# A two-layer feed-forward behind a chunked scan: layer 1's high part rounded by VectorE from ScalarE's result, and the first piece's diagonal copies on VectorE alone

## The chip, the cores and the metric

One core of a Trainium2 chip. The metric is the device time of one execution in microseconds (us), the median of several runs. Of the core's engines the text names TensorE (PE), VectorE (DVE), ScalarE (ACT), GpSimd (POOL) and SyncE (SP), which here issues the data DMAs.

## The reference

Inputs: x (4 x 8 x 768 x 32), decays a (4 x 8 x 768), B and C (4 x 8 x 768 x 16), and the weights of two layers. First comes attention as a decayed linear scan over chunks of 32 positions; then two feed-forward layers over 3072 tokens of 256 values, 2048 hidden ones.

```python
for c in range(nc):                       # chunks of 32 positions
    cum = np.cumsum(la, axis=-1)          # la = log of the clipped decays
    L = np.exp(cum[:, :, :, None] - cum[:, :, None, :]) * causal
    y_intra = np.einsum('bhij,bhjd->bhid', np.einsum('bhin,bhjn->bhij', Cc, Bc) * L, xc)
    y_inter = np.einsum('bhin,bhnd->bhid', Cc, state) * np.exp(cum)[:, :, :, None]
    y[:, :, sl] = y_intra + y_inter
    state = decay_full[:, :, None, None] * state + np.sum(Bx, axis=2)
x = y.transpose(0, 2, 1, 3).reshape(B * S, H * D)
h = x @ w_in1;  x = np.maximum(0.01 * h, h) @ w_out1        # layer 1
h = np.maximum(x @ w_in2, 0.0);  out = (h * h) @ w_out2     # layer 2
```

## The kernel before, in words

**Numbers in two parts.** The layers multiply in a rounded format (`float32r`, fp32r in the rows). Each fp32 number is kept as a high part, rounded to that format, and a low part, what the rounding leaves; a product is three matmuls: low by high, high by high, high by low. So whoever makes an operand makes two: `yh` and `yl` (input of a layer), `gh` and `gl` (hidden values), `wh` and `wl` (weights).

**Weights.** They arrive as 8-byte numbers, four matrices (`1i`, `1o`, `2i`, `2o`: layer, in or out) of eight chunks each. A chunk is loaded (`load_w`), turned into fp32 by two ACT operations (L130, L133, `split_w`) and two DVE operations (L141, L142, `split_w1`), then cut into parts by ACT (L153) and DVE (L154, `split_w2`). Weight chunks are worked on from the start to some 160 us.

**Pieces, blocks, tiles.** The 3072 tokens are twelve pieces of 256, three to each of four sequences. `scan_piece` (L308) is a generator that scans one piece in some twenty steps: scales and decays (`decays`, L189; `from_start`, L195), a block-diagonal copy of each operand (`diag`, L314, into `kbd`, `xbh`, `xbl`, `sbd`), matmuls into `S` and `Y`, the states `stt` (L213) carried from piece to piece, their halves `shl` (L382, L384), transposed to `t16` (L386), and at the end `yh` (L397, ACT) and `yl` (L398, DVE). `diag` moves four quadrants of 32 partitions: in piece 0 by engines, two on DVE and two on ACT for each of the four operands; in later pieces by four SP DMAs (L318). Behind that a block is one piece (the first four) or two (the last four). A block passes layer 1, then layer 2, in the written order `ORDER`, whose entries are layer and block: block 0, 1 and 2 of layer 1, then block 0 of layer 2, and so on in turn.

A block's hidden values come in tiles of 128 x 512 (`t`, `gh`, `gl`, three buffers each), 8 to a one-piece block, 96 to a layer. `hmm` (L417) makes the 12 matmuls of a tile into PSUM (three buffers), `act` (L429) makes the hidden values of it on ACT and DVE, and `omm` (L445), two or three tiles later (`LAG`), multiplies them by the out weights: lines 453 and 454 with `gh`, L458 with `gl`. `finish` (L460) hands the result on as layer 2's `yh`, `yl` (L466, L467) or writes it out (L471, L472).

In layer 1 `act` is: ACT reads PSUM twice, once rounding to `gh` (L435), once to fp32 `t` (L436); DVE forms `gl` as their difference (L441). In layer 2 ACT makes `t` (L438), DVE squares it (L439), ACT rounds it to `gh` (L440), DVE forms `gl` (L441).

**What sets the order.** The program interleaves these steps by its own counters: `step_to(due(...))` advances the scan so that a block's pieces are ready in time, `w_step` the weight chunks. The scales of a later sequence (`sequence_scales`, L269) are stepped beside the scan: five loads of `all` (L276, one buffer, on SP) and a square of each on ACT (L235). A tile framework then gives each engine one static queue, which it works through in order; where its scheduler puts an instruction depends on the others, so an edit of a line also moves lines that it does not touch.

Of the kernel before, what the change touches and what calls it, by code (L numbers as in the profile page):

```python
# [15 lines left out]
AF = mybir.ActivationFunctionType  # L16
# [29 lines left out]
def ssd_moe_kernel(ctx: ExitStack, tc: tile.TileContext, in1, in2, w1i, w1o, w2i, w2o, out):  # L46
# [6 lines left out]
    nc = tc.nc  # L53
# [254 lines left out]
    def scan_piece(p, tiles, get_y):  # L308
# [5 lines left out]
        def diag(dst, src):  # L314
            for h in range(4):
                d, v = dst[quad[h], :, h, :], src[quad[h]]
                if p > 0:
                    nc.sync.dma_start(d, v)  # L318
                else:
                    (nc.vector.tensor_copy if h < 2 else nc.scalar.copy)(d, v)  # L320

        him = sp.tile([P, U, T], F16, tag="f0", name="him")
        ch = sp.tile([P, U, T], F16, tag="f2", name="ch")
# [6 lines left out]
        cl = sp.tile([P, U, T], F16, tag="f3", name="cl")  # L330
        nc.vector.scalar_tensor_tensor(kmx, bt_t, sb, him, ALU.mult, ALU.subtract)
        diag(kbd, kmx)
        xh = sp.tile([P, U, D], F16, tag="xh", name="xh")
        nc.scalar.activation(xh, x_t, AF.Copy, scale=sx)
# [5 lines left out]
        xl = sp.tile([P, U, D], F16, tag="xl", name="xl")  # L340
        nc.vector.scalar_tensor_tensor(xl, x_t, sx, xh, ALU.mult, ALU.subtract)
        diag(xbh, xh)
        yield
        mkh = sp.tile([P, U, T + N], F16, tag="mkh", name="mkh")
        mkl = sp.tile([P, U, T + N], F16, tag="mkl", name="mkl")
        S = pz.tile([P, U, T], F32, tag="S", name="S")
        for u in range(U):
# [6 lines left out]
            mk[:, :, T:], b_t, sb, lt[:, :, T - 1 : T].to_broadcast([P, U, N]), ALU.mult, ALU.mult  # L354
        )
        diag(xbl, xl)
        yield
        nc.vector.scalar_tensor_tensor(mk[:, :, :T], S, kk, lt, ALU.mult, ALU.mult)
# [47 lines left out]
    class Phase:  # L406
# [22 lines left out]
        def act(self, ms):  # L429
            n, hp = self.n, self.h  # L430
            t = ap_.tile([P, 512], F32, tag="t", name="t", bufs=3)
            gh, gl = (ap_.tile([P, 512], F32R, tag=x, name=x, bufs=3) for x in ("gh", "gl"))
            if self.layer == 1:

                nc.scalar.activation(gh, hp, AF.Lrelu)  # L435
                nc.scalar.activation(t, hp, AF.Lrelu)  # L436
            else:
                nc.scalar.activation(t, hp, AF.Relu)  # L438
                nc.vector.tensor_tensor(t, t, t, ALU.mult)  # L439
                nc.scalar.copy(gh, t)  # L440
            nc.vector.tensor_tensor(gl, t, gh.bitcast(F32), ALU.subtract)  # L441
            for j, m in enumerate(ms):
                self.g[m] = gh[:, j * n : j * n + n], gl[:, j * n : j * n + n]
# [176 lines left out]
```

## Time and profile before

| | us |
|---|---|
| median of 3 runs | 636.08 (635.6 to 636.33) |
| the profiled execution | 637.78 |
| its span (first to last instruction) | 636.1 |
| PE busy | 586.2 (92%) |
| DVE busy, 687 instructions | 402.6 (63%) |
| ACT busy, 678 instructions | 372.9 (59%) |
| mean granted clock of PE | 0.99 of full speed |

The span is cut into stretches below, since the shares over the whole do not hold in each: the first layer-1 block starts at 31.65 us, all weight chunks are done near 160, and the scan ends much before the layers do. Where a row gives an idle time in brackets, it is the engine's idle time just ahead of the row's instruction, with the releaser that the trace infers.

### The profile page before, as it was taken

To read this page: it belongs to the slowest core of one execution; us is meant where nothing else is said; L and a number is where in the kernel's file an instruction comes from. 1 tells how busy PE (TensorE), PEld (TensorE's weight loads), DVE (VectorE), ACT (ScalarE), POOL (GpSimd) and SP (SyncE) were. 2 spreads that over 40 slices of the span, in tenths; PEclk is the share of its full clock that TensorE was granted. 3 is DMA by queue.
4 is the path that set the end of the run, shared out by engine and by line. 5 is a ranking of instruction groups with operands and counts; after the bars stand their busy time and mean duration, and the time that the engine had idled before them with its cause. 6 is when DMAs were issued, how large, how long until landed. Compare 5 with 4: busy or idle time off the path is not lost.

```text
span 636.1 us, 11298 instructions
## 1 busy us (share of the span) xinstructions
PE 586.2 (92%) x4434; PEld 516.9 (81%) x4434; DVE 402.6 (63%) x687; ACT 372.9 (59%) x678; POOL 5.2 (1%) x14
## 2 busy tenths in 40 slices
PE   0297698999989999999999999999999999999997
PEld 0287698989989888899988888888888888888885
DVE  6999999995558664576564576564565322555553
ACT  6999998876555545545545555455544433544442
POOL 3000000000000000000000000000000000000000
PEclk9999898999989999999999999999999999999999
DMA  7886565555351412202212212212000000000000
GB/s 272 275 291 195 139 205 98 174 124 127 105 94 40 74 51 26 50 35 42 51 51 26 49 36 25 51 67 26 9 1 9 34 1 1 0 2 0 34 1 33
DMA packets 111396, 46.47 MB, mean 73 GB/s; under 512 B 94320, under 2 KB 101104, under 8 KB 111344
## 3 DMA queue, kind: packets, MB, share of 16 engines
q1 hardware_dynamic: 111344, 45.76, 27.8%
q8 instruction: 35, 0.57, 0.4%
q14 instruction: 17, 0.14, 0.1%
HBM read 36.83 MB, written 3.15 MB: 63 GB/s over the span
## 4 chain that ended last, share of the span: by engine, by line
PE 76%; ACT 9%; DVE 6%; DMA 6%; issue 2%; SPq 1%; DVEq 0%; ACTq 0%
PE o L453 12%; PE hp L425 12%; PE hp L427 12%; PE hp L426 12%; PE o L458 12%; PE o L454 12%; DMA all<-in 2%; DMA in<-in 2%; ACT wst L130 1%; ACT wst L133 1%; ACT sq L235 1%; SPq L318 1%; ACT t L436 1%; ACT gh L435 1%; DVE e L195 1%
## 5 line engine op out<-in xcount | busy, mean ns | idle before, releaser
L441 DVE TENSOR_TENSOR gl<-t,gh 128x512 fp32r<-128x512 f32 x192 | 132.3, 689 | 139.5 <-ACT t L436 85.9
L435 ACT ACTIVATE gh<-hp 128x512 fp32r<-128x512 f32 x96 | 57.2, 596 | 84.1 <-PE o L454 75.6
L425 PE MATMUL hp<-yl,wh1i 128*128 128x256 f32 (+1 forms) x256 | 89.5, 350 | 10.8 <-DVE yl L398 4.6
L440 ACT CAST gh<-t 128x512 fp32r<-128x512 f32 x96 | 59.5, 620 | 66.3 <-DVE t L439 56.2
L439 DVE TENSOR_TENSOR t<-t 128x512 f32<-128x512 f32 x96 | 66.2, 689 | 43.4 <-ACT t L438 43.1
L438 ACT ACTIVATE t<-hp 128x512 f32<-128x512 f32 x96 | 57.4, 598 | 56.7 <-PE hp L427 54.5
L453 PE MATMUL o<-gh,wl1o 128*128 128x256 f32 (+1 forms) x256 | 84.9, 347 | 4.5 <-DVE wl1o L154 3.6
L426 PE MATMUL hp<-yh,wh1i 128*128 128x256 f32 (+1 forms) x256 | 88.6, 346 | 0.0
L427 PE MATMUL hp<-yh,wl1i 128*128 128x256 f32 (+1 forms) x256 | 88.4, 345 | 0.0
L426 PE MATMUL hp<-yh,wh2i 128*128 128x256 f32 (+1 forms) x256 | 86.0, 336 | 0.0
L425 PE MATMUL hp<-yl,wh2i 128*128 128x256 f32 (+1 forms) x256 | 86.0, 336 | 0.0
L427 PE MATMUL hp<-yh,wl2i 128*128 128x256 f32 (+1 forms) x256 | 86.0, 336 | 0.0
L453 PE MATMUL o<-gh,w2o 128*128 128x256 f32 (+1 forms) x256 | 83.6, 343 | 1.6 <-DVE yl L467 1.5
L454 PE MATMUL o<-gh,wh1o 128*128 128x256 f32 (+1 forms) x256 | 83.0, 340 | 0.0
L454 PE MATMUL o<-gh,w2o 128*128 128x256 f32 (+1 forms) x256 | 81.9, 336 | 0.0
L425 PEld LDWEIGHTS hp<-yl,wh1i 128*128 128x128 f32 x256 | 51.3, 200 | 16.7 <-DVE ss L256 3.8
L458 PE MATMUL o<-gl,wh1o 128*128 128x256 f32 (+1 forms) x256 | 60.5, 339 | 0.0
L458 PE MATMUL o<-gl,w2o 128*128 128x256 f32 (+1 forms) x256 | 60.3, 336 | 0.0
L453 PEld LDWEIGHTS o<-gh,wl1o 128*128 128x128 f32 x256 | 48.9, 191 | 10.6 <-DVE wl1o L154 4.7
L436 ACT ACTIVATE t<-hp 128x512 f32<-128x512 f32 x96 | 57.1, 594 | 0.0
L426 PEld LDWEIGHTS hp<-yh,wh1i 128*128 128x128 f32 x256 | 51.3, 200 | 5.1 <-issue 0.3
L427 PEld LDWEIGHTS hp<-yh,wl1i 128*128 128x128 f32 x256 | 51.0, 199 | 5.1
(123 smaller groups left out, 984.8 us busy)
## 6 DMA issues: line engine op xcount, KB each, us to landing
in<-in SPq DMA_DIRECT2D x12, 640.0 KB, 4.6
in<-in SPq DMA_DIRECT2D x12, 512.0 KB, 3.4
all<-in SPq DMA_DIRECT2D x15, 384.0 KB, 3.7
wst<-w1i SPq DMA_DIRECT2D x8, 512.0 KB, 7.9
wst<-w1o SPq DMA_DIRECT2D x8, 512.0 KB, 5.8
wst<-w2o SPq DMA_DIRECT2D x8, 512.0 KB, 5.1
wst<-w2i SPq DMA_DIRECT2D x8, 512.0 KB, 4.7
out_t<-ob SPq DMA_DIRECT2D x8, 256.0 KB, 2.2
```

Of the source, the lines that this page charges most:

```text
L425: nc.tensor.matmul(hp, wh, self.xl[:, :, k], start=(k == 0), stop=False)
L426: nc.tensor.matmul(hp, wh, self.xh[:, :, k], start=False, stop=False)
L427: nc.tensor.matmul(hp, wl, self.xh[:, :, k], start=False, stop=(k == KI - 1))
L435: nc.scalar.activation(gh, hp, AF.Lrelu)
L436: nc.scalar.activation(t, hp, AF.Lrelu)
L438: nc.scalar.activation(t, hp, AF.Relu)
L439: nc.vector.tensor_tensor(t, t, t, ALU.mult)
L440: nc.scalar.copy(gh, t)
L441: nc.vector.tensor_tensor(gl, t, gh.bitcast(F32), ALU.subtract)
L453: nc.tensor.matmul(self.o[d], wl, gh, start=(m == 0), stop=False)
L454: nc.tensor.matmul(self.o[d], wh, gh, start=False, stop=False)
L458: nc.tensor.matmul(self.o[d], wh, gl, start=False, stop=(m == KO - 1))
```

## The change

In `act`, for layer 1, ACT reads PSUM once, into `t`, and DVE rounds `t` to `gh` by a copy into the rounded format. In `diag`, for piece 0, all four quadrants go by DVE copies. No other line is touched.

```diff
@@ L317 (diag, piece 0)
-                    (nc.vector.tensor_copy if h < 2 else nc.scalar.copy)(d, v)
+                    nc.vector.tensor_copy(d, v)
@@ L432 (Phase.act, layer 1)
-                nc.scalar.activation(gh, hp, AF.Lrelu)
                 nc.scalar.activation(t, hp, AF.Lrelu)
+                nc.vector.tensor_copy(gh, t)
```

So 96 ACT operations of 128 x 512 and 8 of 32 x 512 leave ACT, and as many come to DVE. In the changed kernel L435 is the ACT operation that makes `t`, and L436 the DVE copy, named CAST. The queues move as well; three places follow.

DVE, in the scan of piece 0 (`in_117` holds that piece's products, `e_179` its decays from the start). One piece of the difference, - before, + after:

```order
 L320 COPY kbd<-kmx 32x16x32 x2
 L189 SCALAR_TENSOR_TENSOR lt<-in_117,delta 128x512
-L320 COPY xbl<-xl 32x16x32
+L320 COPY kbd<-kmx 32x16x32 x2
+L320 COPY xbh<-xh 32x16x32 x2
 L353 SCALAR_TENSOR_TENSOR in_117<-in_116,sc,lt 128x16x16
-L320 COPY xbl<-xl 32x16x32
+L320 COPY xbl<-xl 32x16x32 x4
+L358 SCALAR_TENSOR_TENSOR in_117<-S,kk,lt 128x16x32
 L368 SCALAR_TENSOR_TENSOR ql<-e_179,sc,qh 128x512
```

The copies that ACT made stand in DVE's queue, among DVE's own, all ahead of the first `yl`.

DVE, in front of block 2's `yl` (the third L398), of before and then of the change (`in_1280` and `in_1279` are inputs of piece 3):

```order
L441 TENSOR_TENSOR gl<-t,gh 128x512
L350 TENSOR_TENSOR e_1561<-in_1279,e_1561 128x512
L341 SCALAR_TENSOR_TENSOR xl<-in_1279,sc,xh 128x512
L142 SCALAR_TENSOR_TENSOR wst<-wst 128x512
L205 MEMSET d1s 128x32
L141 SCALAR_TENSOR_TENSOR wst<-wst 128x512
L331 SCALAR_TENSOR_TENSOR kmx<-in_1280,sc,him 128x512
L398 SCALAR_TENSOR_TENSOR yl<-Y,fac,yh 128x512
```

```order
L436 CAST gh<-t 128x512
L154 TENSOR_TENSOR wl2i<-wst,wh2i 128x2x256
L441 TENSOR_TENSOR gl<-t,gh 128x512
L141 SCALAR_TENSOR_TENSOR wst<-wst 128x512
L195 SCALAR_TENSOR_TENSOR e_1561<-in_1280,d1e 128x512
L142 SCALAR_TENSOR_TENSOR wst<-wst 128x512
L341 SCALAR_TENSOR_TENSOR xl<-in_1279,sc,xh 128x512
L350 TENSOR_TENSOR e_1561<-in_1279,e_1561 128x512
L154 TENSOR_TENSOR wl2i<-wst,wh2i 128x2x256
L398 SCALAR_TENSOR_TENSOR yl<-Y,fac,yh 128x512
L331 SCALAR_TENSOR_TENSOR kmx<-in_1280,sc,him 128x512
```

Each layer-1 `gl` has a CAST ahead of it now, and one operation that stood in front of this `yl`, L331, stands behind it.

ACT, around piece 4's `shl`, of before and then of the change (`ob` is layer 2's output of a block, `sq` the square of a load `all`, `d1s` and `stt` are the states of piece 4):

```order
L471 COPY ob<-o_1984 128x256
L325 ACTIVATE ch<-in_2509,sc 128x512
L235 ACTIVATE sq,mx<-all 128x768
L435 ACTIVATE gh<-hp 128x512
L436 ACTIVATE t<-hp 128x512
L435 ACTIVATE gh<-hp 128x512
L436 ACTIVATE t<-hp 128x512
L377 ACTIVATE d1s<-Y 128x32x8
L235 ACTIVATE sq,mx<-all 128x768
L382 CAST shl<-stt 128x16x16
L207 ACTIVATE d1s<-stt 128x32
```

```order
L471 COPY ob<-o_1984 128x256
L235 ACTIVATE sq,mx<-all 128x768
L435 ACTIVATE t<-hp 128x512 x2
L235 ACTIVATE sq,mx<-all 128x768
L377 ACTIVATE d1s<-Y 128x32x8
L382 CAST shl<-stt 128x16x16
L207 ACTIVATE d1s<-stt 128x32
L235 ACTIVATE sq,mx<-all 128x768
L435 ACTIVATE t<-hp 128x512
```

Before, two squares stand between `ob` and `shl`, the second of them directly ahead of `shl`; now the two stand ahead of `d1s`, and a third stands behind `shl`.

## Rows read from the trace of the kernel before

**Rows 1.** page, its sections 1 and 4: engines' busy time, and the chain that ended last

```profile
PE 586.2 (92%) x4434; PEld 516.9 (81%) x4434; DVE 402.6 (63%) x687; ACT 372.9 (59%) x678; POOL 5.2 (1%) x14
...
PE 76%; ACT 9%; DVE 6%; DMA 6%; issue 2%; SPq 1%; DVEq 0%; ACTq 0%
```

**Rows 2.** busy time by stretch: length, then us busy (instructions) of each engine, granted clock, DMA

```profile
12.28:30.85 18.57, 4.26 (x112) 3.90 (x112) 17.95 (x34) 18.46 (x33) 0.00 (x0) 1.00 0.78 262
30.85:72.68 41.83, 31.85 (x308) 29.46 (x308) 41.40 (x89) 41.81 (x85) 0.00 (x0) 1.00 0.74 225
72.68:104.00 31.32, 28.91 (x308) 28.22 (x308) 30.00 (x61) 28.82 (x55) 0.00 (x0) 0.95 0.64 167
...
104.90:160.00 55.10, 53.56 (x542) 53.15 (x543) 45.33 (x76) 40.83 (x77) 0.00 (x0) 0.97 0.51 129
220.00:632.00 412.00, 411.91 (x2589) 347.98 (x2587) 219.22 (x336) 200.47 (x352) 0.00 (x0) 1.00 0.12 26
```

**Rows 3.** timeline of PE: start, us, line, operation, idle before and releaser

```profile
73.46 0.39 PE L425 MATMUL hp<-yl,wh1i 128*128 128x256 f32 x1 [3.68 <-DVE ss L256]
...
104.89 0.51 PE L425 MATMUL hp<-yl,wh1i 128*128 128x256 f32 x1 [2.16 <-DVE yl L398]
...
137.70 0.39 PE L453 MATMUL o<-gh,w2o 128*128 128x256 f32 x1 [1.54 <-DVE yl L467]
...
179.75 0.18 PE L393 MATMUL Y<-qh,sbd 128*128 128x32 f16 x1 [2.93 <-DMA sbd<-t]
```

**Rows 4.** timeline of DVE before the second and third `yl`

```profile
71.55 1.21 DVE L189 TENSOR_TENSOR_SCAN lt<-in,delta 128x512 f32<-128x512 f32 x1
72.68 0.72 DVE L398 SCALAR_TENSOR_TENSOR yl<-Y,fac,yh 128x512 fp32r<-128x512 f32 x1
...
100.26 0.68 DVE L441 TENSOR_TENSOR gl<-t,gh 128x512 fp32r<-128x512 f32 x1
100.86 0.68 DVE L350 TENSOR_TENSOR e<-in,e 128x512 f32<-128x512 f32 x1
...
103.34 0.74 DVE L331 SCALAR_TENSOR_TENSOR kmx<-in,sc,him 128x512 f16<-128x512 f32 x1
104.00 0.74 DVE L398 SCALAR_TENSOR_TENSOR yl<-Y,fac,yh 128x512 fp32r<-128x512 f32 x1
```

**Rows 5.** busy time by stretch, PE alone: us, us busy, granted clock, DMA

```profile
104.90:108.90 4.00, 4.00 (x21) 0.57 0.42 44
137.00:141.00 4.00, 3.30 (x26) 1.00 0.56 114
179.70:183.70 4.00, 3.95 (x47) 0.57 0.39 43
```

**Rows 6.** groups of ACT: count, us busy, mean ns; the last from 104.9 to 160 alone

```profile
L435 ACT ACTIVATE gh<-hp 128x512 fp32r<-128x512 f32 x96 | 57.2, 596 | 84.1 <-PE o L454 75.6 <-PE hp L427 8.4
L320 ACT COPY kbd<-kmx 32x512 f16<-32x512 f16 x2 | 1.2, 611 | 0.0
...
L435 ACT ACTIVATE gh<-hp 128x512 fp32r<-128x512 f32 x9 | 5.4, 601 | 4.3 <-PE hp L427 4.1
```

**Rows 7.** groups of DVE over the whole span

```profile
L441 DVE TENSOR_TENSOR gl<-t,gh 128x512 fp32r<-128x512 f32 x192 | 132.3, 689 | 139.5 <-ACT t L436 85.9 <-ACT gh L440 53.1
L186 DVE TENSOR_SCALAR in<-in 128x496 f32<-128x496 f32 x12 | 4.9, 411 | 0.0
L320 DVE COPY kbd<-kmx 32x512 f16<-32x512 f16 x2 | 0.6, 283 | 0.0
```

**Rows 8.** timeline of ACT ahead of piece 4's `shl`

```profile
168.15 0.39 ACT L377 ACTIVATE d1s<-Y 128x256 f32<-128x256 f32 x1
172.54 0.84 ACT L235 ACTIVATE sq<-all 128x768 bf16<-128x768 f32 x1 [4.01 <-DMA all<-in]
173.39 0.66 ACT L382 CAST shl<-stt 128x256 f16<-128x256 f32 x1
```

**Rows 9.** timeline of SP's DMA queue, piece 4's `sbd`

```profile
175.54 2.61 SPq L318 DMA_DIRECT2D sbd<-t  x4
```

## The prediction

> **What bounds the kernel now.** The page's first lines give TensorE (PE) 586.2 of the span's 636.1 us, VectorE (DVE) 402.6 and ScalarE (ACT) 372.9, and the chain that ended last is 76% PE [rows 1]. Read over the whole span, that says PE. The busy times by stage [rows 2] say it differently. From 220 us on PE is busy 411.91 of 412.00, and DVE and ACT have slack (219.22 and 200.47). Before 104 us it is the other way: between 30.85 and 72.68 PE works 31.85 of 41.83 us, while DVE is busy 41.40 and ACT 41.81. Over the three stretches from 12.28 to 104.00 DVE is idle 0.62, 0.43 and 1.32, together 2.37 us. In that front DVE and ACT scan the first pieces and split weights, and PE waits.
>
> So the question is when PE is fed, and the timeline of PE shows it [rows 3]. The first matmuls of layer 1's blocks 1 and 2 begin at 73.46 and 104.89, after idle times of 3.68 and 2.16 us. The releaser of the latter is the `yl` of the block's piece (L398), the last instruction of its scan; the former is put down to a small DVE operation just behind a `yl`. DVE's timeline [rows 4] shows the third and second `yl` at 104.00 and 72.68, with the next operation in front of each starting 0.66 and 1.13 us earlier, that is, without a gap. Hence the start of block 2 is the sum of all that stands in DVE's queue ahead of the third `yl`. Behind block 2 PE seldom waits; what it waits for longest there is one DMA at 179.75, for 2.93 us [rows 3]. That stall is the second place that matters.
>
> A further cost hangs on such idle times. In the four microseconds after the gaps of 2.16 and 2.93 the granted clock is 0.57, and after a gap of 1.54 at 137.70 it is 1.00 [rows 5]. At 0.57 in the mean, 4 us do the work of 2.3: each of the two gaps costs 1.7 us more.
>
> **The change part by part.** *What leaves ACT*: 96 `gh` (L435) of 596 ns and the eight copies of the first piece (L320), 611 ns each [rows 6]. What of this lies behind 220 us is worth nothing, since PE is the bound there. In the front ACT loses 8 x 0.61 = 4.9 us, and up to 0.60 us a tile. That pays only so far as DVE waited for ACT, at most the 2.37 us of idle time above.
>
> *What comes to DVE, the diagonal copies.* The copies it already makes take 283 ns [rows 7]. Eight more, at 0.28, are +2.24 us, all ahead of the first `yl`.
>
> *What comes to DVE, the cast of `t` to `gh`.* The trace of before has no such DVE operation. Nearest above: L441, of the same size and in SBUF, but with two inputs, 689 ns. Nearest below: L186, one input, fp32 in SBUF, 496 columns wide, 411 ns [rows 7]. As L441 is followed after 0.60 us (100.26 to 100.86 in [rows 4]), 0.09 overlap, so in a full queue the cast costs between 0.33 and 0.60. I take 0.34, since one input and its memory are what it shares with L186. The Trainium skill, "VectorE: DVE Perf Modes", section "The perf-mode tier table", has copies of fp32 in SBUF run at twice the rate of a two-input operation; by that the sum is the one below, and by L441's row the third `yl` would come another 16 x 0.26 = 4.2 us later.
>
> *The sum at each `yl`.* I counted DVE's queue ahead of each, before and after the change. First `yl`: +2.24, less two L142 that have moved behind it (0.60 each): +1.0. Second: +2.24, plus 8 casts (2.72), less one scan of a later piece, L189 (1.13), that has moved behind it: +3.8. Third: +2.24, plus 16 casts (5.44), less two L141 and one L142 (1.80) and one L331 (0.66): +5.2. Of this the relieved ACT can give back up to 2.37. How much is not shown; I take half, 1.2. **Block 2 starts 4.0 us later, between +2.9 and +5.2**, near 108.9. Behind its start PE's order is the same but for one tile, so the delay stays. The weight splits that move back are layer 2's, whose first block comes only after block 2.
>
> From block 2 to 220 us DVE gets another cast a tile. It is busy 45.33 of 55.10 us from 104.90 to 160 [rows 2] and PE runs there nearly without a wait, so the casts of that stretch (9 tiles of layer 1 by ACT's groups [rows 6], 3.1 us) and the few splits that have moved back fit into its 9.8 idle ones; ACT gives up as many `gh` there, so `t` is not later. I count this at nothing. If the cover is gone, the wait at 137.70 (DVE's `yl`, L467) grows by a cast or two, +0.3 to +0.7.
>
> *What comes back at the DMA stall.* PE waits at 179.75 for `sbd` of piece 4. Its chain stands in ACT's timeline [rows 8]: ACT is ready for `shl` (L382) after `d1s` at 168.15, yet the next in its queue is a square whose load (`all`, one buffer) arrives at 172.54, after 4.01 us of idling; `shl` runs at 173.39, and SP issues the four `sbd` at 175.54 [rows 9]. In the changed order that square stands behind `shl`, and on SP one load fewer stands ahead of `sbd`. Then `shl` is set by the later of `d1s`, which ends at 168.54 and has one DVE scan behind it, and the previous square; so up to 4 us are to be had. But the previous square's load is now issued behind the two output DMAs, and other operations of ACT have moved too. I take 1.5 to 3 us of the 4. A gap of 2.93 becomes 0 to 1.4; with 1.4 or less the clock stays (as after 1.54). The return lies between 0 and 2.93 + 1.7 = 4.6; I take 2.0, under half, as the queue shift is certain and its size is not.
>
> Sum: +4.0 - 2.0 = +2.0 on a profiled execution of 637.78 us, which lies 1.7 us above the median of 636.08. Against the median that is 638.1; **I say 638.0**.
>
> **The rivals.**
>
> *A. The front's loss stays, a part comes back* (the forecast, slower): between +2.9 - 1.6 and +5.2 - 0.9, that is +1.3 to +4.3: 637.4 to 640.4. For it: DVE without a gap to 72.68 [rows 2]. The Trainium skill has a rule that speaks against the change in the same sense: "Perfetto Trace Analysis", section "Optimizing Scalar/DVE Operations", says that where VectorE is saturated, giving some of its work to ScalarE may make sense; the change does the reverse where VectorE is at 41.40 of 41.83.
>
> *B. Given back at the stall* (no change): +4.0 in front, and 3 to 4.6 back, as the gap falls to nothing and takes the clock's loss with it: -0.6 to +1.0, so about 636. For it: the 4.01 us of ACT's idle time before `shl` are there by queue order alone, and the changed order has no such square in that place.
>
> *C. The stall goes and ACT was the real bound of the front* (faster). One mechanism decides: if all of `shl`'s wait vanishes, PE gets 2.93 us and the clock's 1.7 back, 4.6; against a front of +2.9, all of DVE's idle time won back, that is -1.7: 634.4, and at best another 1.5, 632.9, where the wait at 137.70 goes too. It decides from +3.3 in front downward. For it: ACT is busy 41.81 of 41.83 in the same stretch as DVE, and loses more (4.9 us and up to 0.60 a tile) than DVE gains. Against it: DVE's idle time is all that ACT can have cost, 2.37, and the queue grew by 5.2.
>
> *D. The cast does not get the short price.* At L441's rate it adds 0.26 x 16 = 4.2 to the third `yl`, +9.4 or, less 1.2, +8.2 in front; less 2.0 at the stall that is +6.2: 642.3, to 644 where nothing comes back. For it: `gh` is of another type (fp32r), and every DVE operation of the trace that writes it runs at the long price, all of them with two inputs. Against: those of one input and fp32 take 411 ns.
>
> That the change doesn't do what it says is no case of its own: casts and copies stand in DVE's order.
>
> **How the numbers follow.** About 0.2% (1.3 us) is what a measurement of this kernel can tell from no change. Chances: A 0.40, B 0.30, C 0.17, D 0.13. Faster is C, 0.17; slower is A and D, 0.53; the same is B, 0.30. The likeliest case alone spans 637.4 to 640.4. The range leaves out somewhat over half of C (below 634.5) and the far part of D (above 643, 0.06), about 0.16 together: 634.5 to 643.0.
>
> **What the profile after would show.** Right: DVE's cast near 420 ns; the second and third `yl` near 76 and 108; DVE idle for 1 to 2 us only between 12 and 108; PE unchanged from 220 us plus the delay on, with the same 412 us of work; the stall before piece 4's L393 under 1.5 us with the granted clock at 1.00 behind it. Wrong: a third `yl` at or before 105 would mean that ACT was the bound; casts of about 690 ns mean D; a stall of some 3 us before piece 4 means that the queue's order there did not count; and a new wait of over 1 us on PE behind 110 us, for `gl` or `gh`, would mean that the cast's cover was too thin.

## The result, and the profile after

The changed kernel took **642.01 us** in the median of four executions (640.52 to 644.21), against 635.84 for the kernel before: a ratio of **1.0102, interval 1.0068 to 1.0136**. A second set of six executions gave 1.0079 (1.0052 to 1.0107), median 641.98. It is slower, by about 5 to 6 us, as forecast in sign; 638.0 was the forecast, 634.5 to 643.0 the range.

The two profiled executions are nearer to each other than the medians: 640.52 us after, 637.78 before. Their difference of 2.74 us is what the rows can account for directly; the rest is a matter of the granted clock, below.

The page after, sections 1 and 4 (as [rows 1]):

```profile
PE 586.6 (92%) x4434; PEld 516.4 (81%) x4434; DVE 439.5 (69%) x791; ACT 325.5 (51%) x574; POOL 5.1 (1%) x14
...
PE 71%; DVE 14%; DMA 7%; ACT 5%; issue 2%; SPq 1%; DVEq 0%; ACTq 0%
```

ACT has lost 47 us of work and DVE gained 37. PE's work is the same, but DVE's share of the chain that ended last went from 6% to 14%. Busy time by stretch (as [rows 2]; the first three stretches end at the first, second and third `yl`):

```profile
12.28:31.70 19.42, 4.86 (x114) 4.42 (x114) 19.04 (x39) 16.75 (x33) 0.00 (x0) 1.00 0.73 245
31.70:77.98 46.28, 33.48 (x306) 29.92 (x306) 44.30 (x99) 39.84 (x75) 0.00 (x0) 0.96 0.74 220
77.98:109.30 31.32, 28.39 (x308) 28.01 (x308) 30.98 (x66) 22.61 (x42) 0.00 (x0) 0.95 0.57 147
...
224.00:636.00 412.00, 410.67 (x2580) 346.90 (x2578) 243.12 (x398) 172.20 (x289) 0.00 (x0) 1.00 0.12 26
```

ACT, busy 41.81 of 41.83 us before in the second stretch, now idles 6.4 us there, and 8.7 in the third. DVE's idle times in the three are 0.38, 1.98 and 0.34, together 2.70; before they were 0.62, 0.43 and 1.32, together 2.37. So between these two profiles the relief of ACT gave DVE nothing back on balance; other profiles of before say it differently, below. From 224 us on PE's work is the same (the window reaches 1.3 us past its last matmul); under it DVE has 24 us more and ACT 28 less.

The three `yl` in DVE's timeline (as [rows 4]), and the waits of PE's timeline (as [rows 3]):

```profile
31.70 0.75 DVE L398 SCALAR_TENSOR_TENSOR yl<-Y,fac,yh 128x512 fp32r<-128x512 f32 x1
...
77.98 0.74 DVE L398 SCALAR_TENSOR_TENSOR yl<-Y,fac,yh 128x512 fp32r<-128x512 f32 x1
...
109.29 0.75 DVE L398 SCALAR_TENSOR_TENSOR yl<-Y,fac,yh 128x512 fp32r<-128x512 f32 x1
```

```profile
78.78 0.39 PE L425 MATMUL hp<-yl,wh1i 128*128 128x256 f32 x1 [2.26 <-DVE ss L256]
...
110.10 0.38 PE L425 MATMUL hp<-yl,wh1i 128*128 128x256 f32 x1 [2.93 <-DVE yl L398]
...
142.17 0.38 PE L453 MATMUL o<-gh,w2o 128*128 128x256 f32 x1 [0.78 <-DVE yl L467]
...
183.74 0.18 PE L393 MATMUL Y<-qh,sbd 128*128 128x32 f16 x1 [1.64 <-DMA sbd<-t]
```

Against [rows 3] and [rows 4]: the second `yl` is 5.3 us later, the third 5.3, and block 2's start 5.2 (110.10 against 104.89). By 142.17 the lag is 4.5, since the wait for L467 fell from 1.54 to 0.78; by 169.03 it is 5.3 again, chiefly by a longer wait for ACT's `ob` (1.49 us, 0.86 before); at 183.74 it is 4.0, the wait for `sbd` being 1.64 instead of 2.93. The last step is the clock (as [rows 5]):

```profile
110.10:114.10 4.00, 4.00 (x22) 0.61 0.47 49
142.00:146.00 4.00, 3.79 (x29) 1.00 0.54 89
183.70:187.70 4.00, 3.96 (x58) 1.00 0.38 41
```

Behind the shorter wait at 183.74 the clock stays at its full level, which saves the 1.7 us that before lost there: 4.0 less 1.7 is 2.3, and with small differences behind it the span is 2.6 longer.

### The profile page after: what moved, and what is told of

It reads as the page before. It is cut to its first block, busy times and chain, and to the rows that moved or that the text cites. A ratio compares the mean times of both kernels' runs of the same rounds, so it can differ in the third digit from the quotient of the medians.

```text
span 638.7 us, 11339 instructions
## 1 busy us (share of the span) xinstructions
PE 586.6 (92%) x4434; PEld 516.4 (81%) x4434; DVE 439.5 (69%) x791; ACT 325.5 (51%) x574; POOL 5.1 (1%) x14
## 4 chain that ended last, share of the span: by engine, by line
PE 71%; DVE 14%; DMA 7%; ACT 5%; issue 2%; SPq 1%; DVEq 0%; ACTq 0%
PE o L453 11%; PE hp L425 11%; PE hp L426 11%; PE hp L427 11%; PE o L458 11%; PE o L454 11%; DMA in<-in 2%; DVE gl L441 2%; DMA wst<-w1o 2%; DVE wst L141 1%; DVE wst L142 1%; ACT sq L235 1%; DMA all<-in 1%; DVE e L195 1%; DVE lt L189 1%
## 5 line engine op out<-in xcount | busy, mean ns | idle before, releaser
L441 DVE TENSOR_TENSOR gl<-t,gh 128x512 fp32r<-128x512 f32 x192 | 132.4, 690 | 55.1 <-ACT gh L440 48.6
L435 ACT ACTIVATE t<-hp 128x512 f32<-128x512 f32 x96 | 57.3, 597 | 121.3 <-PE hp L427 121.2
L436 DVE CAST gh<-t 128x512 fp32r<-128x512 f32 x96 | 40.5, 422 | 58.5 <-PE o L454 48.6
```

What stands on the lines that cost most here:

```text
L436: nc.vector.tensor_copy(gh, t)
```

## The experiments

Each starts from the kernel before unless it says otherwise. The identity to hold them against: the third `yl`'s shift is the work added to DVE's queue ahead of it (counted from the order, at durations of before and 0.34 us a cast) plus the change of DVE's idle time from the first `kmx` (12.28) to that `yl`, 2.37 us before.

| kernel | queue, us | DVE idle, us (change) | third `yl` later by | block 2 starts | ratio, interval |
|---|---|---|---|---|---|
| changed | +5.2 | 2.7 (+0.3) | 5.3 | 110.10 | 1.0102 (1.0068 to 1.0136) |
| diagonal copies alone | +2.8 | 5.2 (+2.9) | 5.8 | 110.70 | 1.0088 (1.0060 to 1.0116) |
| cast alone | +3.0 | 1.8 (-0.6) | 1.9 | 106.79 | 1.0039 (1.0019 to 1.0060) |
| cast behind block 2 alone | 0.0 | 3.4 (+1.1) | 1.1 | 106.00 | 1.0001 (0.9983 to 1.0018) |
| two copies (`kbd`) | +1.8 | 4.0 (+1.6) | 3.2 | 107.95 | 1.0063 (1.0040 to 1.0086) |
| six copies (the others) | +1.7 | 3.8 (+1.5) | 3.1 | 107.94 | 1.0048 (1.0027 to 1.0069) |
| all copies, cast to block 2 | +5.2 | 2.6 (+0.2) | 5.0 | 109.84 | 1.0090 (1.0075 to 1.0105) |

It holds within 0.5 us in every row. It is bookkeeping: DVE's time is work or idle time, so it says where a delay sits, and not why the idle time arose.

**The diagonal copies alone.**

```diff
-                    (nc.vector.tensor_copy if h < 2 else nc.scalar.copy)(d, v)
+                    nc.vector.tensor_copy(d, v)
```

> The diagonal copies on VectorE alone; layer 1's high part as before. Theory Q (VectorE's queue ahead of the third yl sets block 2's start): the queue is 2.8 us longer there, of which the relieved ScalarE gives back up to half, so block 2 starts at 106 to 108 (104.89 before) and the time is 637 to 639. Theory G (what costs is the late gh: PE waits 7.3 us for the cast's result, in seven waits): no cast, so no change, 635 to 637, and block 2 at 105 or earlier.

Measured: median 642.12 us of six, block 2 at 110.70. Later than theory Q, and the opposite of theory G: this half, with 2.2 us of work, costs as much as the whole change. The idle time it makes, in DVE's timeline and then in ACT's:

```profile
36.00 1.29 DVE L154 TENSOR_TENSOR wl1i<-wst,wh1i 128x512 fp32r<-128x512 f32 x2 [1.11 <-ACT wh1i L153]
...
39.83 1.29 DVE L154 TENSOR_TENSOR wl1i<-wst,wh1i 128x512 fp32r<-128x512 f32 x2 [0.72 <-ACT wh1i L153]
...
83.23 0.69 DVE L441 TENSOR_TENSOR gl<-t,gh 128x512 fp32r<-128x512 f32 x1 [1.28 <-ACT t L436]
```

```profile
34.73 0.69 ACT L130 ACTIVATE wst<-wst 128x512 f32<-128x512 f32 x1 [2.29 <-DMA wst<-w1o]
```

DVE waits for ACT's weight parts, and ACT stands at a weight load that has not come. Further on DVE waits for a `t`, just after PE's late start of block 1.

**The cast alone.**

```diff
-                nc.scalar.activation(gh, hp, AF.Lrelu)
                 nc.scalar.activation(t, hp, AF.Lrelu)
+                nc.vector.tensor_copy(gh, t)
```

> Layer 1's high part rounded by VectorE; the diagonal copies as before. Theory Q: the queue ahead of the third yl is 3.0 us longer; block 2 starts at 106.5 to 108.5, time 637.5 to 640, so this and the other half share the loss. Theory G: the whole loss is here, about 642, with waits of PE for gh of about 7 us in all between the first and the second block.

Measured: median 639.40 us of twelve, ratio 1.0039 (2.5 us), block 2 at 106.79: as theory Q has it. PE does wait for `gh` (0.67, 1.50 and 1.52 us in the longest), but between the starts of blocks 0 and 1, where DVE's `yl` sets block 1's start in any case. Theory G falls. Here the relief of ACT does pay: DVE's idle time falls by 0.6.

**The cast behind block 2 alone.**

```diff
-                nc.scalar.activation(gh, hp, AF.Lrelu)
+                if self.t0 < 3 * TP:
+                    nc.scalar.activation(gh, hp, AF.Lrelu)
                 nc.scalar.activation(t, hp, AF.Lrelu)
+                if self.t0 >= 3 * TP:
+                    nc.vector.tensor_copy(gh, t)
```

> Layer 1's high part rounded by VectorE only from block 3 on (72 of the 96 casts); blocks 0 to 2 and the diagonal copies as before. Theory Q: behind block 2 the casts are covered; the front's queue is within 1.3 us of before; time 634.5 to 637.5. If the casts behind the front have a price of their own (late gh in the steady state): 638 or more, with PE waits for gh behind 110 us.

Measured: 636.12 us, ratio 1.0001. In the front DVE's order is that of before, row by row (my count of +1.3 ahead of the run was wrong). Still block 2 starts 1.1 us later than in the profile of before. At block 1's start, 73.59, PE's clock was already at its half level, and longer than before (there 1.00, 0.57 and 1.00 in these stretches), so `t` came later to DVE; and the wait for `sbd` shrinks. PE by stretch, one stretch of before beside it, and PE's timeline:

```profile
70.00:74.00 4.00, 0.41 (x2) 0.71 0.95 297
74.00:78.00 4.00, 4.00 (x20) 0.50 0.66 126
78.00:82.00 4.00, 4.00 (x34) 0.94 0.12 13
```

```profile
74.00:78.00 4.00, 4.00 (x23) 0.57 0.68 131
```

```profile
106.00 0.55 PE L425 MATMUL hp<-yl,wh1i 128*128 128x256 f32 x1 [2.17 <-DVE yl L398]
...
179.47 0.18 PE L393 MATMUL Y<-qh,sbd 128*128 128x32 f16 x1 [1.05 <-DMA sbd<-t]
```

So 72 of the 96 casts cost nothing that can be measured, the shorter wait for `sbd` included. And the third `yl` of one and the same front varies: 104.0 in the profile of before, 105.1 here, 105.4 in the control below; DVE's idle time ahead of it is 2.37, 3.42 and 3.71 us. The table's rows, each of one profile and all held against the earliest of these three, are to be read with that: against the other two, every shift is 1.1 to 1.4 us smaller.

**The changed kernel once more.** No edit.

> The changed kernel once more, for its spread: its profiled execution was 2.7 us over that of before, its median 6.2. Theory K (the rest is the granted clock, which falls behind some of PE's longer idle times in one execution and not in another): the executions lie between 640 and 645, the longer the lower their mean clock (0.979 to 0.990), block 2 starts at 110 +- 0.5 in any profile, and a profile with a lower mean clock shows more stretches of 3.4 us at half clock, behind idle times of 1.3 to 2 us. If the front itself varies instead: the start of block 2 moves by 2 to 4 us between profiles at the same number of such stretches.

Measured: six executions, 639.27 to 642.80. Block 2 starts at 110.13 in this profile (110.10 in the first) after the same idle time of 2.93 us; block 2's start is the same. What differs is the clock, and the wait for `sbd`:

```profile
110.10:114.10 4.00, 3.97 (x18) 0.50 0.47 49
114.10:118.10 4.00, 4.00 (x28) 0.73 0.87 257
184.60:188.60 4.00, 3.98 (x49) 0.59 0.45 48
```

```profile
184.62 0.19 PE L393 MATMUL Y<-qh,sbd 128*128 128x32 f16 x1 [2.09 <-DMA sbd<-t]
```

In this execution the half clock lasts into the second four microseconds, where in the first it ended within the first four; and the wait for `sbd` is 2.09 us, not 1.64, and is followed by the half clock again. This execution's span is 641.0 us (mean clock 0.984), 2.3 longer than the first (638.7, 0.990). Theory K holds in the main: one execution, that of the highest mean clock (0.994), lies below its 640, and the half clock also lasts longer, and not only comes oftener.

**Two copies, and the other six.**

```diff
-                    (nc.vector.tensor_copy if h < 2 else nc.scalar.copy)(d, v)
+                    (nc.vector.tensor_copy if h < 2 or dst is kbd else nc.scalar.copy)(d, v)
```

The second kernel has `dst is not kbd` in that place.

> Of the eight diagonal copies only the two of kbd, the first ones, move to VectorE; the cast stays away. The diagonal copies alone moved block 2's start by 5.8 us where VectorE's queue had grown by 2.8. Theory N (the loss goes by the copies' time on VectorE and what that delays, weight loads above all): a quarter of it or the queue's +1.8, block 2 at 106 to 107, time 636.5 to 638. Theory S (the first scan's start: PE's S waits for kbd, at 15.93 against 15.07): most of it, block 2 at 109 or later, 640 to 642.

> The other six diagonal copies on VectorE, kbd as before. Theory N: three quarters of the loss of all eight, block 2 at 108 to 110, time 639 to 641, with ScalarE waiting over 1 us for a load of w1o near 34 us. Theory S: S at 15.1 as before, block 2 at 105 to 107, 636 to 638.

Measured: both start block 2 at the same moment, 107.95 and 107.94; medians 639.07 and 639.60. Theory S falls: PE's first S stood at 16.02 in the one and at 15.02 in the other. Theory N falls as it was put, since two copies cost as much as six and their sum (1.1%) is more than all eight cost (0.9%). The wait of over 1 us for a load of w1o near 34 us did not come either; with the six copies ACT waits 1.07 us there, at 35.47, for an `hp`. What is left is the bookkeeping of the table: each has a queue 1.7 to 1.8 us longer, as the order came out, and 1.5 to 1.6 us more of idle time. Why two copies bring as much idle time as six is not shown.

**All copies, the cast for blocks 0 to 2 alone.** The edit is the changed kernel's, with the two conditions of the late cast exchanged.

> The diagonal copies on VectorE, and the cast on VectorE for blocks 0 to 2 alone (24 of 96); behind them ScalarE reads PSUM twice as before. Theory Q: all of the change's loss, block 2 at 109.5 to 110.7, time 640.5 to 643. If the other 72 casts had a price of their own: 637 to 640.

Measured: 642.12 us, 1.0090, block 2 at 109.84. The whole loss is made in the front, by 8 copies and 24 casts.

**ACT's copies on GpSimd.**

```diff
-                    (nc.vector.tensor_copy if h < 2 else nc.scalar.copy)(d, v)
+                    (nc.vector.tensor_copy if h < 2 else nc.gpsimd.tensor_copy)(d, v)
```

> ScalarE's eight diagonal copies go to GpSimd instead, so ScalarE is relieved by 4.9 us and VectorE's queue gets none of it; the cast stays away. If ScalarE's relief is worth anything in the front: block 2 at 103 to 104.9, 633.5 to 636. If ScalarE's relief is worth nothing, since VectorE bounds: within 1 us of before. If a copy on GpSimd takes over 1 us: S and Y of piece 0 wait for it, the weight splits of VectorE go ahead meanwhile, and the time is 637 to 640.

Measured: 643.16 us, ratio 1.0118 (1.0094 to 1.0143), block 2 at 113.14, worse than the change. In DVE's and GpSimd's timelines:

```profile
13.40 1.27 DVE L320 COPY kbd<-kmx 32x512 f16<-32x512 f16 x2
```

```profile
13.22 1.30 POOL L320 COPY kbd<-kmx 32x512 f16<-32x512 f16 x2 [7.26 <-DVE kmx L331]
```

DVE's two copies, at the same moment as GpSimd's, take 1.27 us where they took 0.58 before. None of the three expectations holds. Of the 8.3 us by which the third `yl` is late, 1.8 are a longer queue, as the order came out, some 2.6 are DVE's slower operations, and 3.8 are idle time (6.2 in all), most of it behind the second `yl`, where PE's mean granted clock is 0.83 (0.95 before). So the kernel doesn't show what ACT's relief alone is worth.

**More buffers for weight loads.** To test whether the late weight loads make DVE's new idle time: the changed kernel, and the kernel before as control, with two buffers that nothing else needs until the last weights.

```diff
-        if nm == "2o" and c >= 5:
+        if nm == "1o" and c < 2 or nm == "2o" and c >= 5:
             st = yp.tile([P, 2, 256], I64, tag="y2", name="wst")
```

> The changed kernel; its first two chunks of w1o are loaded into two buffers that stand free until the end of the weights, so that their loads don't wait for VectorE's L154 to release a buffer. VectorE's queue ahead of the second and third yl is the changed kernel's (+3.8 and +5.2 us). Theory L (the copies also delay the release of weight buffers, the loads come late, ScalarE waits for them and VectorE for ScalarE: 1.98 us of idle time before the second yl instead of 0.43): the idle time falls to 0.3 to 0.8, the second yl comes at 76.5 to 77, block 2 at 108.5 to 109.5, and the time is 0.6 to 1.5 us under the changed kernel's, 640 to 641.5. If the waits have another cause: second yl at 78 or later, time 641.5 to 643.

> The kernel before with the same two buffers: the control, VectorE's queue unchanged. Theory L: VectorE idles 0.43 there before, so at most that can be won: block 2 at 104.4 to 105, time within 1 us of before. If late loads cost the kernel before something too: block 2 before 104, under 635.

Measured on the changed kernel: 642.06 us, ratio 1.0089, block 2 at 110.47, second `yl` at 78.33. Theory L falls. The loads do come earlier; ACT's and DVE's timelines:

```profile
28.68 0.67 ACT L130 ACTIVATE wst<-wst 128x512 f32<-128x512 f32 x1 [0.58 <-DMA wst<-w1o]
...
36.16 0.60 ACT L435 ACTIVATE t<-hp 128x512 f32<-128x512 f32 x1 [0.77 <-PE hp L427]
```

```profile
38.53 0.69 DVE L154 TENSOR_TENSOR wl1i<-wst,wh1i 128x512 fp32r<-128x512 f32 x1 [1.13 <-ACT wh1i L153]
...
42.28 0.69 DVE L154 TENSOR_TENSOR wl1i<-wst,wh1i 128x512 fp32r<-128x512 f32 x1 [1.25 <-ACT wh1i L153]
```

ACT's wait for the load is down from 1.47 us to 0.58, and in its place ACT waits in its queue for `hp` of block 0's tiles, with the weight parts behind that; DVE idles 2.39 us in the second stretch, not less. Which order of ACT's queue would avoid both wasn't tried.

The control is the kernel before to within its interval: 636.01 us, 1.0000 (0.9979 to 1.0020). Its profile shows how far the clock, and the loads that PE and ACT wait for, move the same work. VectorE's order is that of before, row by row; PE's half clock begins earlier and lasts longer around block 1's start (before: 0.57 from 74 to 78 us), and block 2 starts at 106.27, 1.4 us later than before and behind the 104.4 to 105 expected. Yet the span is 633.5, 2.6 below the profiled span of before:

```profile
70.00:74.00 4.00, 0.40 (x2) 0.66 0.92 289
74.00:78.00 4.00, 4.00 (x20) 0.50 0.67 129
106.20:110.20 4.00, 3.93 (x33) 1.00 0.41 43
178.50:182.50 4.00, 3.94 (x58) 1.00 0.38 42
```

After the same idle time of 2.16 us as before, the clock stays at its full level in this execution, and also behind the wait for `sbd`, here 1.55 us and not 2.93.

**The cast on ScalarE.**

```diff
-                nc.scalar.activation(gh, hp, AF.Lrelu)
                 nc.scalar.activation(t, hp, AF.Lrelu)
+                nc.scalar.copy(gh, t)
```

> PSUM read once by ScalarE into t, and ScalarE rounds t to gh from SBUF; the diagonal copies as before. So VectorE gets nothing and ScalarE keeps its count: what the single PSUM read is worth by itself. VectorE's queue ahead of the third yl is 1.3 us longer by order. Theory Q: block 2 at 105 to 106.2, time 635.5 to 637.5. If gh one ScalarE operation later (0.5 us behind t) costs PE a wait a tile: 638 or more.

Measured: 637.82 us, 1.0030 (1.0016 to 1.0045), block 2 at 106.69: 1.8 us slower, just beyond theory Q on both counts, and without a wait a tile. With ACT's count unchanged and a queue 1.3 us longer, nothing is won by reading PSUM once.

**A try at a shorter queue.** Layer 2's low weight parts on GpSimd:

```diff
-        nc.vector.tensor_tensor(l, w, h.bitcast(F32), ALU.subtract)
+        (nc.gpsimd if nm[0] == "2" else nc.vector).tensor_tensor(l, w, h.bitcast(F32), ALU.subtract)
```

> Theory Q in the other direction, and a try at a kernel that beats both: the kernel before, with layer 2's low weight parts (L154, 16 operations, six of them ahead of the third yl) formed by GpSimd, which is idle. Other splits move up, so VectorE's queue ahead of the third yl is 1.3 us shorter. Theory Q: block 2 at 103.4 to 104.9, time 634 to 636, a gain of 0 to 1.5 us. If a GpSimd operation beside VectorE's slows either so far that weights come late: PE waits of over 1 us for wl2i behind 115 us, 637 or more.

Measured: 647.81 us, 1.0176 (1.0151 to 1.0202), block 2 at 110.63, though the queue is 1.3 us shorter and DVE idles 0.7 less than before. Theory Q's 103.4 to 104.9 is missed, since it took DVE's durations as unchanged. GpSimd's group, DVE's groups, and one meeting of the two in their timelines:

```profile
L154 POOL TENSOR_TENSOR wl2i<-wst,wh2i 128x512 fp32r<-128x512 f32 x8 | 11.8, 1485 | 91.6 <-ACT wh2i L153 83.7 <-DMA xbh<-xh 7.9
...
91.14 3.23 POOL L154 TENSOR_TENSOR wl2i<-wst,wh2i 128x512 fp32r<-128x512 f32 x2 [1.44 <-ACT wh2i L153]
```

```profile
L441 DVE TENSOR_TENSOR gl<-t,gh 128x512 fp32r<-128x512 f32 x192 | 135.8, 707 | 139.8 <-ACT t L436 86.2 <-ACT gh L440 53.1
...
L141 DVE SCALAR_TENSOR_TENSOR wst<-wst 128x512 int32<-128x512 int32 x32 | 25.2, 804 | 0.0
```

```profile
91.38 1.81 DVE L441 TENSOR_TENSOR gl<-t,gh 128x512 fp32r<-128x512 f32 x1
```

Beside GpSimd's operation a `gl` takes 1.81 us, not 0.69; L141's mean rises from 684 ns to 804. The lengthening of DVE's operations is the 7.8 us that the identity lacks here (a queue of -1.3 and idle time of -0.7 against a third `yl` 5.8 later). Behind block 2 PE waits 5.0 us for the `yl` of L467 (1.54 before), which is most of the rest. No version that beats the kernel before was found.

## Why the prediction was right, and where it was off

**What bounds the front: right.** DVE's queue ahead of the third `yl`, and the idle time in it, set block 2's start. The sums of the queue alone were +1.0, +3.8 and +5.2; measured were +0.85, +5.3 and +5.3. That the third agrees is in part luck: DVE's idle time grew by 1.5 us before the second `yl` and shrank by 1.0 before the third, and against the two other profiles of the same front (105.1 and 105.4) the third `yl` is only 4.2 and 3.9 us late. With the cast held back to behind block 2 the loss is gone; with copies and cast in the front alone it is all there.

**The cast's price: right.** Its group in the changed kernel:

```profile
L436 DVE CAST gh<-t 128x512 fp32r<-128x512 f32 x96 | 40.5, 422 | 58.5 <-PE o L454 48.6 <-ACT t L435 7.6 <-PE o L458 1.8
```

422 ns, near the price of L186 [rows 7] and not that of L441; rival D is out by this row. In a full queue the next operation starts 0.33 us behind a cast (41.90 to 42.23), where 0.34 was taken.

**"Of this the relieved ACT can give back up to 2.37 ... I take half, 1.2": not settled.** In the third stretch DVE's idle time did fall, from 1.32 us (2.25 and 2.54 in the two other profiles of the same front) to 0.34 and, in the second profile of the changed kernel, 0.12. But in the second stretch it rose, from 0.43 (0.54 and 0.54) to 1.98 (2.36). Between the two profiles of the table the net is +0.3, nothing won, and that is the 1.2 us by which block 2 started later than forecast (110.1, not 108.9). Against the two other profiles of the front of before, in which PE's half clock lasted longer and DVE idled 3.42 and 3.71 us, the changed kernel's 2.70 and 2.87 are 0.6 to 1.0 less, and block 2 starts 4.1 and 3.8 us later, near the 4.0 of the forecast. So the term lies between a loss of 0.5 and a gain of 1.0, by which profiles are held together. The rise in the second stretch stands in all of them. With diagonal copies on DVE the first weight parts come later, and ACT, relieved, stands at what is late next: loads of w1o and block 0's `hp`:

```profile
33.94 0.72 ACT L130 ACTIVATE wst<-wst 128x512 f32<-128x512 f32 x1 [1.47 <-DMA wst<-w1o]
...
37.16 0.60 ACT L435 ACTIVATE t<-hp 128x512 f32<-128x512 f32 x1 [0.33 <-PE hp L427]
```

```profile
39.48 1.29 DVE L154 TENSOR_TENSOR wl1i<-wst,wh1i 128x512 fp32r<-128x512 f32 x2 [0.53 <-ACT wh1i L153]
...
44.00 0.69 DVE L154 TENSOR_TENSOR wl1o<-wst,wh1o 128x512 fp32r<-128x512 f32 x1 [0.96 <-ACT wh1o L153]
```

I had bounded the term by 0 and 2.37; this rise is a negative side that I excluded without a reason. That the loads alone are its cause was tested and is not so; which order of ACT's and DVE's work makes it stays open.

**"The return ... I take 2.0": its size is luck, its cause not shown.** As argued, the square that stood before `shl` stands behind it. Measured against PE, which is 5.2 us late, `shl` is 3.0 us earlier (175.61 against 173.39), the upper end of what I took. What is late next is DVE, where one scan (L189) now runs until 177.17, so that `shl`'s second half (L384) starts 0.8 us behind the first, and another scan has moved in front of the transpose:

```profile
174.39 0.37 ACT L377 ACTIVATE d1s<-Y 128x256 f32<-128x256 f32 x1
175.61 0.68 ACT L382 CAST shl<-stt 128x256 f16<-128x256 f32 x1 [0.85 <-DVE stt L213]
```

```profile
177.62 1.21 DVE L195 TENSOR_TENSOR_SCAN e<-in,d1e 128x512 f32<-128x512 f32 x1
178.75 0.68 DVE L386 STREAM_TRANSPOSE t<-shl 128x512 f16<-128x512 f16 x1
```

So the wait fell by 1.3 us only, and the clock's 1.7 came back in the first profile but not in the second, nor in that of the copies with the front's cast (2.07 us, ended by a `t` of ACT by the profile, granted clock 0.59 behind it). The return is 3.0 in one execution and about 0.8 in the others.

And the stall of 2.93 us that all this is held against is no fixed base. The control with other buffers and the diagonal copies alone have ACT's order around `shl` as before, with the square directly ahead of it. In ACT's timeline and PE's, first of the control, then of the diagonal copies alone:

```profile
170.75 0.84 ACT L235 ACTIVATE sq<-all 128x768 bf16<-128x768 f32 x1 [2.02 <-DMA all<-in]
...
178.56 0.18 PE L393 MATMUL Y<-qh,sbd 128*128 128x32 f16 x1 [1.55 <-DMA sbd<-t]
```

```profile
176.12 0.84 ACT L235 ACTIVATE sq<-all 128x768 bf16<-128x768 f32 x1 [1.51 <-DMA all<-in]
...
184.31 0.18 PE L393 MATMUL Y<-qh,sbd 128*128 128x32 f16 x1 [1.41 <-DMA sbd<-t]
```

ACT waits 2.02 and 1.51 us for the square's load there, not 4.01, and PE's stall is 1.55 and 1.41, no longer than the 1.64 and 2.09 of the changed order. So a stall of this size comes without the queue shift too, and what the shift itself gives back is not shown.

**The reference of the sum.** I took the difference of the profiles for that of the medians. The profiled execution of before was 1.8 us above the median of 68 executions that came with these runs (635.99); the first one of the changed kernel was 1.5 us below that of its ten (641.98). The mean granted clock was 0.979 to 0.994 in those ten, 0.986 in the mean, and 0.985 to 0.997 in the 68, 0.991 in the mean; at 0.984 to 0.985 the changed kernel's four spans are 639.6 to 641.0 and the two of before 637.0 and 637.9; at 0.990 its one span is 638.7 against 633.9 in the mean of eleven, at 0.994 637.5 against 633.9 in the mean of ten. So at an equal clock the change costs some 2 to 5 us, mostly more than the 2.74 between the profiles, and the rest goes with more, and longer, stretches at half clock. That this is because the changed kernel has more waits of PE of 1 to 3 us in the front is likely, but wasn't tested by itself. The profile of before was also long at its stall, as said.

**Rivals, range and signs.** A happened, beyond its upper end (640.4): forecast +2.0, measured +5 to +6. That the range still holds 642.01 is luck: it reached to 643.0 for rival D, which is out. B needed 3 to 4.6 us back at the stall; 3.0 came in one profile, with more lost in front than B allowed, and 0.8 in the others. C is excluded: ACT idled 17.8 us in the front and the third `yl` came 5.3 later. Of the signs, the cast's price came as said, and PE behind 220 us is as forecast. The second and third `yl` (77.98 and 109.29, not near 76 and 108), DVE's idle time (2.70 us, not 1 to 2) and the stall (1.64 and 2.09, not under 1.5) did not. Behind 110 us no new wait came, and the one that grew is that for `ob`, at 169.03, from 0.86 to 1.49 us.

## What to carry to other kernels

Where two engines are both full, expect work moved from one to the other to cost its whole time at the receiver, and the relieved engine's slack to give back no more than the receiver waited for it; here that was between -0.5 and +1.0 us of 5.2. Bound what may be won back below zero, too, since a static queue that is reordered makes waits of its own. Count the queue ahead of the instruction that feeds the bound, and look at the place where work falls before its amount: 72 casts behind the front cost nothing, 24 casts and 8 copies in it cost 1%. And when a kernel's waits are near the length at which the clock falls in one execution and not in the next, one profile of each kernel is no measure of their medians; before a stall is counted as something to win back, see in a second profile of the same kernel whether it is there.

## What was not expected of the hardware

After PE's idle time of 2.93 us, at the same place of the same kernel, the granted clock was at its half level (1.2 of 2.4 GHz) for most of 4 us in one execution (0.61 in the mean) and for well over 4 in another (0.50, then 0.73). After one of 2.16 us it fell in one execution [rows 5] and not in the control with other buffers (1.00).

GpSimd beside VectorE cost more than its own time: an operation of two inputs in SBUF took 1.81 us beside one of GpSimd (0.69 alone), and copies of 32 x 512 in 16 bits 0.63 (0.28). The Trainium skill, "SBUF — State Buffer", section "SBUF: two separate sides", describes a port pair that these two engines share and that one of them holds for a whole instruction while the other is blocked; the durations agree with that.
